# A reordered start of the first batch, and w_in permuted while it is cast so that w_out loads in long runs

## The chip, the cores and the metric

The kernel runs on one core of one Trainium2 chip. The metric is the device time of one execution in microseconds (us). PE is the tensor engine's matmul side, DVE is VectorE, ACT is ScalarE, POOL is GpSimd and SP is SyncE, which issues the transfers.

## The reference, cut to what matters

For each of 8 batches and 8 heads (576 positions, head size 64) an attention without a score matrix, then one feed-forward block over all 4608 tokens:

```python
q_s = softmax(q, axis=-1)            # over the head's 64 features
k_s = softmax(k, axis=2)             # over the 576 positions
kv  = einsum('bhsd,bhse->bhde', k_s, v)
x   = einsum('bhsd,bhde->bhse', q_s, kv)   # then (tokens, 512)
h   = x @ w_in                       # 512 -> 2048
g   = 0.5 * h * (1 + erf(h / sqrt(2)))
out = g @ w_out                      # 2048 -> 512
```

A permutation of w_in's 2048 columns permutes the columns of h and g. If w_out's rows are permuted alike, the output is the same.

## The kernel before

The kernel works on a chunk of 512 tokens at a time: a first projection (`h_phase`, 64 matmuls of 512 columns), Gelu on ACT, a second projection (`y_phase`, 64 matmuls). Attention for a later chunk runs between the matmuls. Only chunk 0 has nothing to hide behind: before its first projection, q, k, v and w_in must have landed and gone through this chain. Idle matmuls (`warm`) stand at the head so that PE is at full pace when the real work comes.

```python
    warm(30)
    table(AF.Exp)
    exp_q(0, parts=2)
    ...                                   # [cut: exponentials of k on ACT, q's normalisation]
    tp_step(0, 0)                         # transposes of q, pairs 0 and 1
    warm(5)
    ...                                   # [cut: casts of v; w_in blocks 0 and 1 on POOL]
    kv_pair(0, 0)
    tp_mm(0, 1)                           # transposes of q, pairs 2 and 3
    norm_pair(0, 0, "v")
    tp_evac(0, 1, "s")                    # their eviction, on ACT
    kv_pair(0, 1)
    norm_pair(0, 1, "v")
    x_step(0, 0)                          # x product of pair 0 and its eviction on DVE
    kv_pair(0, 2)
    kv_pair(0, 3)
    x_step(0, 1, "s")
    norm_pair(0, 2, "s")                  # half on DVE, half on ACT
    norm_pair(0, 3, "s")
    table(AF.Gelu)
    h_phase(0, {
        0: [lambda: cast_wi(2, wi[2], "v")],
        2: [lambda: cast_wi(3, wi[3], "v")],
        ...
    }, groups={0: 2}, pre={
        1: [lambda: x_step(0, 2)],        # before the matmuls on xT's second slice
        2: [lambda: x_step(0, 3)],
    })
```

w_in comes in five blocks of 256, 256, 512, 512 and 512 columns; POOL casts the first two to bf16 and DVE the others. w_out comes in four blocks of 512 rows, 1 MB each. In a partition, a block's four rows are 128 rows apart, so each run of DRAM is one row, 2 KB.

```python
        o = wi_bf[:, :, wi_off[i]:wi_off[i] + n]
        ...
                nc.vector.tensor_copy(out=o[:, c:c + d], in_=w[:, c:c + d, 0:n])
    ...
        src = moe_w_out[i * 512:(i + 1) * 512, :].rearrange("(c p) f -> p c f", p=128)
```

The softmax here doesn't subtract the row's maximum and nothing guards it: scores larger than these inputs give would overflow.

## Time and profile before

| | kernel before |
|---|---|
| median of the first 3 runs | 286.33 us (286.24 to 286.64) |
| span in the profile | 284.4 us |
| PE busy | 276.6 us, 97% |
| first projection of chunk 0 runs without a gap from | 17.68 us |
| second projection of chunk 0 starts at | 30.19 us |
| last eviction starts at | 281.03 us |

Read the table from the bottom: from the second projection's start to the last eviction there are 250.84 us, almost all of it matmuls at one per 0.216 us. What is left is the start, and that is where this change works. The lines of the profile are in the prediction below.

### The profile page before, as it was taken

How to read it: one execution, taken by the hardware profiler on the slowest of the kernel's cores; microseconds unless marked ns; L12 is line 12 of the kernel's file. 1: busy time of each engine (PE TensorE's matmuls, PEld its weight loads, DVE VectorE, ACT ScalarE, POOL GpSimd, SP SyncE). 2: the span in 40 equal slices, each digit the busy share in tenths (PEclk: the TensorE clock that was granted, in tenths of full speed). 3: DMA queues.
4: the chain of work that ended last, by engine and by line, in shares of the span. 5: the costliest groups of instructions: out<-in, count | busy, mean ns of one | idle time of the engine just before them, and what ended most of it. 6: DMA issues, size and time to landing. Idle time of an engine off the chain costs nothing.

```text
span 284.4 us, 3842 instructions
## 1 busy us (share of the span) xinstructions
PE 276.6 (97%) x1484; PEld 131.1 (46%) x1511; DVE 119.4 (42%) x239; ACT 159.7 (56%) x266; POOL 38.6 (14%) x34
## 2 busy tenths in 40 slices
PE   8989999999999999999999999999999999999995
PEld 3534455445445445444544454445444444444443
DVE  7664388028696454354434532453225111110012
ACT  4876595779565934694368526872576165017400
POOL 5830033002020050005000500040001300000000
PEclk9999999999999999999999999999999999999999
DMA  7999999999529939922993199517500600120033
GB/s 239 378 383 387 372 388 309 308 298 233 143 62 268 297 92 246 248 96 88 233 271 102 74 212 277 140 74 170 127 0 37 184 2 0 74 76 0 0 74 76
DMA packets 58593, 50.05 MB, mean 176 GB/s; under 512 B 26704, under 2 KB 48464, under 8 KB 58576
## 3 DMA queue, kind: packets, MB, share of 16 engines
q1 hardware_dynamic: 58288, 49.68, 61.1%
q8 instruction: 12, 0.20, 0.3%
q10 hardware_dynamic: 288, 0.13, 0.2%
q14 instruction: 5, 0.04, 0.1%
HBM read 36.70 MB, written 9.44 MB: 162 GB/s over the span
## 4 chain that ended last, share of the span: by engine, by line
PE 91%; DMA 3%; DVE 2%; ACT 2%; issue 1%; DVEq 0%; ACTq 0%
PE ps L376 40%; PE ps L386 40%; PE ps L476 3%; DMA f<-in_k_dram 3%; PE ps L251 2%; PE ps L408 1%; PE ps L346 1%; PE ps L323 1%; DVE xT L356 1%; ACT ek L145 1%; DVE kvbd L212 1%; PE ps L197 1%; PE ps L255 0%; PE ps L288 0%; ACT L145 0%
## 5 line engine op out<-in xcount | busy, mean ns | idle before, releaser
L381 ACT ACTIVATE g<-ps 128x512 bf16<-128x512 f32 x144 | 85.7, 597 | 93.4 <-PE ps L376 93.4
L376 PE MATMUL ps<-xT,wi_bf 128*128 128x512 bf16 x560 | 128.6, 379 | 1.3 <-DVE xT L356 0.3
L386 PE MATMUL ps<-wo_bf,g 128*128 128x512 bf16 x549 | 123.2, 379 | 0.6
L376 PEld LDWEIGHTS <-wi_bf 128*128 128x128 bf16 x576 | 55.3, 98 | 66.0 <-issue 2.8
L386 PEld LDWEIGHTS <-g 128*128 128x128 bf16 x560 | 54.6, 98 | 64.9
L393 DVE COPY y_sb<-ps 128x512 f32<-128x512 f32 x35 | 23.9, 686 | 74.9 <-PE ps L386 74.6
L243 POOL TENSOR_TENSOR e<-e,recq 128x1024 bf16<-128x1024 bf16 (+1 forms) x10 | 27.6, 2761 | 178.8 <-ACT ek L148 95.7
L356 DVE CAST xT<-ps 128x512 bf16<-128x512 f32 x32 | 20.6, 686 | 32.6 <-PE ps L346 22.5
L241 DVE TENSOR_REDUCE qsum<-e 128x16 f32<-128x1024 bf16 (+1 forms) x13 | 21.1, 1624 | 8.4 <-ACT e L145 7.0
L224 DVE CAST v_aug<-f 128x512 bf16<-128x512 f32 x24 | 10.3, 429 | 10.0 <-DMA f<-in_v_dram 9.3
L148 ACT ACTIVATE e<-f 128x512 bf16<-128x512 f32 (+2 forms) x28 | 13.2, 540 | 0.1
L97 ACT ACT_TABLE_LOAD x9 | 11.5, 1283 | 2.8 <-issue 2.6
L273 DVE TENSOR_SCALAR kvbd<-ps,rec 64x64 bf16<-64x64 f32 x48 | 11.6, 280 | 0.8
L476 PE MATMUL ps<-kvbd 128*128 128x512 bf16 x35 | 10.3, 462 | 1.2 <-DVE scr L85 1.2
L148 ACT ACTIVATE ek<-f 128x512 bf16<-128x512 f32 x20 | 10.9, 613 | 0.0
L182 ACT ACTIVATE ek<-f 64x1152 bf16<-64x1152 f32 x8 | 9.3, 1162 | 1.7 <-DMA f<-in_k_dram 1.5
L145 ACT ACTIVATE e<-f 128x1024 bf16<-128x1024 f32 (+1 forms) x7 | 6.8, 990 | 3.2 <-DMA f<-in_q_dram 3.2
L251 PEld LDWEIGHTS <-ek 128*128 128x128 bf16 x96 | 6.8, 97 | 3.2 <-ACT ek L145 0.6
L251 PE MATMUL ps<-v_aug,ek 128*128 128x129 bf16 x96 | 8.1, 220 | 0.1
L467 DVE CAST wo_bf<-w 128x2048 bf16<-128x2048 f32 (+1 forms) x5 | 5.1, 1014 | 5.8 <-DMA w<-in_moe_w_out_dram 5.7
L476 PEld LDWEIGHTS <-kvbd 128*128 128x128 bf16 x35 | 3.9, 116 | 6.6 <-issue 3.2
L216 DVE CAST vr_aug<-f 64x512 bf16<-64x512 f32 x6 | 2.5, 416 | 8.7 <-DMA f<-in_v_dram 8.7
(52 smaller groups left out, 98.6 us busy)
## 6 DMA issues: line engine op xcount, KB each, us to landing
out_dram<-y_sb SPq DMA_DIRECT2D x32, 256.0 KB, 2.4
f<-in_q_dram SPq DMA_DIRECT2D x6, 1024.0 KB, 7.7
f<-in_k_dram SPq DMA_DIRECT2D x6, 1024.0 KB, 10.8
f<-in_v_dram SPq DMA_DIRECT2D x6, 1024.0 KB, 9.6
w<-in_moe_w_in_dram SPq DMA_DIRECT2D x6, 512.0 KB, 8.6
w<-in_moe_w_out_dram SPq DMA_DIRECT2D x3, 1024.0 KB, 12.8
f<-in_k_dram SPq DMA_DIRECT2D x4, 576.0 KB, 8.6
f<-in_v_dram SPq DMA_DIRECT2D x8, 288.0 KB, 8.1
```

Of the source, the lines that this page charges most:

```text
L97: nc.scalar.activation(out=scr[:, 1:2], in_=scr[:, 0:1], func=func)
L148: nc.scalar.activation(out=dst[:, s::4], in_=src[:, u::4], func=AF.Exp)
L241: nc.vector.reduce_sum(out=qsum, in_=eq[:, :, hs, :], axis=AX.X)
L243: eng.tensor_tensor(out=eq[:, :, hs, :], in0=eq[:, :, hs, :], in1=recq.unsqueeze(3).to_broadcast([128, J, w, D]), op=ALU.mult,)
L251: nc.tensor.matmul(ps, st[b]["ek"][:, j, hs, :].rearrange("p h d -> p (h d)"), v_aug[b % 2][:, j, hp, 0:PW], start=(j == 0), stop=False,)
L273: nc.vector.tensor_scalar_mul(out=kvbd[b][pr, hps[i], c * 64:c * 64 + 64], in0=ps[pr, i, c * (D + 1):c * (D + 1) + D], scalar1=rec[pr, i:i ...
L356: nc.vector.tensor_copy(out=st[b]["xT"][:, hp, :], in_=ps)
L376: nc.tensor.matmul(ps, wi_bf[:, dm, t * 128:(t + 1) * 128], xT[:, dm, :], start=(dm == 0), stop=(dm == NDM - 1),)
L381: nc.scalar.activation(out=g[:, t, :], in_=ps, func=AF.Gelu)
L386: nc.tensor.matmul(ps, st[c]["g"][:, t, j * 128:(j + 1) * 128], wo_bf[:, t, :], start=(t == 0), stop=(t == NDF - 1),)
L393: nc.vector.tensor_copy(out=y_sb, in_=ps)
L476: nc.tensor.matmul(ps, zeros[:, 0:128], zeros, start=True, stop=True)
```

## The change

It has two parts. The chain of batch 0 is reordered: the Gelu table is loaded right after k's exponentials, q's second transpose is evicted by DVE instead of ACT, the normalisations of pairs 2 and 3 become one step on DVE, and the evictions of the x products are shared between ACT and DVE. And w_in's columns are permuted inside each block by the cast (column m·r + c goes to c·128 + m, with r = 2 or 4), so that w_out can be loaded with 2 or 4 neighbouring rows per partition, in runs of 4 or 8 KB.

```diff
+    def kv_two(b):                      # both pairs into one PSUM tile
+        ...
+    def norm_two(b):
+        ps = st[b]["kvt"]
+        rec = small.tile([128, 2], FP32, tag="reck")
+        nc.vector.reciprocal(rec, ps[:, :, D])
+        for hh in range(2):
+            pr = slice(hh * 64, hh * 64 + 64)
+            nc.vector.tensor_tensor(
+                out=kvbd[b][pr, 2:4, hh * 64:hh * 64 + 64], in0=ps[pr, :, 0:D],
+                in1=rec[pr].unsqueeze(2).to_broadcast([64, 2, D]), op=ALU.mult,
+            )
     def cast_wi(i, w, eng):
-        o = wi_bf[:, :, wi_off[i]:wi_off[i] + n]
+        r = n // 128
+        o = wi_bf[:, :, wi_off[i]:wi_off[i] + n].rearrange("p d (c m) -> p d c m", c=r)
+        w = w[:, :, 0:n].rearrange("p d (m c) -> p d c m", c=r)
     def load_wo(i, parts=1):
-        src = moe_w_out[i * 512:(i + 1) * 512, :].rearrange("(c p) f -> p c f", p=128)
+        ... # block 0: two halves with (p c) f, c=2
+        src = src.rearrange("(p c) f -> p c f", c=4)
     tp_mm(0, 1)
+    table(AF.Gelu)
     norm_pair(0, 0, "v")
-    tp_evac(0, 1, "s")
     kv_pair(0, 1)
     norm_pair(0, 1, "v")
-    x_step(0, 0)
-    kv_pair(0, 2)
-    kv_pair(0, 3)
+    x_step(0, 0, "s")
+    tp_evac(0, 1)
+    kv_two(0)
     x_step(0, 1, "s")
-    norm_pair(0, 2, "s")
-    norm_pair(0, 3, "s")
-    table(AF.Gelu)
+    norm_two(0)
     h_phase(0, { ... }, pre={
-        1: [lambda: x_step(0, 2)],
-        2: [lambda: x_step(0, 3)],
+        1: [lambda: x_step(0, 2), lambda: x_step(0, 3, "s")],
     })
```

More of the change, by code (lines that the diff above doesn't have):

```diff
@@ L212, in norm_pair @@
                 nc.vector.tensor_scalar_mul(out=dst, in0=ps[pr, 0:D], scalar1=rec[pr, 0:1])
+    def kv_two(b):
+        ps = psum_a.tile([128, 2, 256], FP32, tag="a")
+        st[b]["kvt"] = ps
+        for i in range(2):
+            for n in range(NS):
+                nc.tensor.matmul(
+                    ps[:, i, 0:D + 1], ek_pair[1][:, i, n, :], v_pair[b][:, 2 + i, n, 0:D + 1],
+                    start=(n == 0), stop=(n == NS - 1),
+                )
[8 more added lines that the diff above has]
+                in1=rec[pr].unsqueeze(2).to_broadcast([64, 2, D]), op=ALU.mult,
+            )
     def cast_vr(b):
@@ L448, in cast_wi @@
         n = wi_cols[i]
-        o = wi_bf[:, :, wi_off[i]:wi_off[i] + n]
+        r = n // 128
+        o = wi_bf[:, :, wi_off[i]:wi_off[i] + n].rearrange("p d (c m) -> p d c m", c=r)
+        w = w[:, :, 0:n].rearrange("p d (m c) -> p d c m", c=r)
         if eng == "p":
             for h in range(2):
-                nc.gpsimd.tensor_copy(out=o[:, 2 * h:2 * h + 2], in_=w[:, 2 * h:2 * h + 2, 0:n])
+                nc.gpsimd.tensor_copy(out=o[:, 2 * h:2 * h + 2], in_=w[:, 2 * h:2 * h + 2])
         else:
@@ L455, in cast_wi @@
             for c in range(0, NDM, d):
-                nc.vector.tensor_copy(out=o[:, c:c + d], in_=w[:, c:c + d, 0:n])
+                nc.vector.tensor_copy(out=o[:, c:c + d], in_=w[:, c:c + d])
     def load_wo(i, parts=1):
         w = wst.tile([128, 4, DM], FP32, tag="w")
-        src = moe_w_out[i * 512:(i + 1) * 512, :].rearrange("(c p) f -> p c f", p=128)
+        src = moe_w_out[i * 512:(i + 1) * 512, :]
+        if i == 0:
+            for h in range(2):
+                nc.sync.dma_start(
+                    out=w[:, 2 * h:2 * h + 2],
+                    in_=src[256 * h:256 * h + 256].rearrange("(p c) f -> p c f", c=2),
+                )
+            return w
+        src = src.rearrange("(p c) f -> p c f", c=4)
         n = 4 // parts
```

## The prediction

> **What bounds the kernel now.** I read the page first. Its busy shares, slices and chain of waits name the resource.
>
> ```profile
> PE 276.6 (97%) x1484; PEld 131.1 (46%) x1511; DVE 119.4 (42%) x239; ACT 159.7 (56%) x266; POOL 38.6 (14%) x34
> ...
> PE   8989999999999999999999999999999999999995
> ...
> PE 91%; DMA 3%; DVE 2%; ACT 2%; issue 1%; DVEq 0%; ACTq 0%
> ...
> L381 ACT ACTIVATE g<-ps 128x512 bf16<-128x512 f32 x144 | 85.7, 597 | 93.4 <-PE ps L376 93.4
> L376 PE MATMUL ps<-xT,wi_bf 128*128 128x512 bf16 x560 | 128.6, 379 | 1.3 <-DVE xT L356 0.3
> L386 PE MATMUL ps<-wo_bf,g 128*128 128x512 bf16 x549 | 123.2, 379 | 0.6
> ```
>
> The reader is to see that PE (the tensor engine) is busy in every slice, that 91% of the chain that ended last is PE, and that the two large matmul groups waited 1.3 us and 0.6 us in the whole run. A "busy" PE can still run slowly, so I checked its pace. Gelu activations in batch 0 start at 20.03, 20.89, 21.76, 22.62 and 23.48 us, one per four matmuls: 3.45 us over 16 matmuls, 0.216 us each. That pace never slackens in the phases that follow, with the clock at 9 tenths or more throughout. Next I took busy time by stretches. From 17.7 to 30 us PE is busy 12.25 of 12.30 us, from 30 to 48.2 us 17.84 of 18.20, from 48.2 to 68 us 19.63 of 19.80. So the kernel is a fixed amount of matmul work, 266 us or so, preceded by about 17 us of preparation. Only where that work starts can be moved.
>
> Third, I read PE's timeline from 10 us on, where the change lies. Columns: start, duration, engine, line, operation, how many, and in brackets the idle time before and what ended it.
>
> ```profile
> 12.85 0.45 PE L197 MATMUL ps<-v_aug,ek 128*128 128x65 bf16 x9
> 13.53 0.39 PE L323 MATMUL ps<-qT,kvbd 128*128 128x512 bf16 x1 [0.23 <-DVE kvbd L212]
> 13.76 0.73 PE L197 MATMUL ps<-v_aug,ek 128*128 128x65 bf16 x18
> 14.34 0.39 PE L323 MATMUL ps<-qT,kvbd 128*128 128x512 bf16 x1
> 15.06 0.38 PE L376 MATMUL ps<-xT,wi_bf 128*128 128x512 bf16 x1 [0.33 <-DVE xT L356]
> 15.86 0.39 PE L323 MATMUL ps<-qT,kvbd 128*128 128x512 bf16 x1 [0.42 <-ACT kvbd L210]
> 16.08 0.59 PE L376 MATMUL ps<-xT,wi_bf 128*128 128x512 bf16 x2
> 16.52 0.38 PE L323 MATMUL ps<-qT,kvbd 128*128 128x512 bf16 x1
> ```
>
> L197 is the KV product of a head pair, L323 the product x of a head pair with its queries, L376 the first projection. The four x products (call them x0 to x3) run at 13.53, 14.34, 15.86 and 16.52 us. The first projection takes x0 to x3 in that order, so it is saturated only when x3 has been evicted. The same stretch of the other engines shows why that is late.
>
> ```profile
> 13.05 1.01 ACT L299 COPY qT<-ps 128x1024 bf16<-128x1024 bf16 x1 [0.16 <-PE ps L288]
> 13.71 0.58 DVE L212 TENSOR_SCALAR kvbd<-ps,rec 64x64 bf16<-64x64 f32 x2
> 14.26 1.18 POOL L452 CAST wi_bf<-w 128x512 bf16<-128x512 f32 x2 [0.84 <-DMA w<-in_moe_w_in_dram]
> 14.32 0.69 DVE L356 CAST xT<-ps 128x512 bf16<-128x512 f32 x1
> 15.49 0.63 ACT L210 ACTIVATE kvbd<-ps,rec 64x64 bf16<-64x64 f32 x2
> 16.14 1.28 ACT L97 ACT_TABLE_LOAD   x1
> 16.28 1.34 DVE L356 CAST xT<-ps 128x512 bf16<-128x512 f32 x2 [0.50 <-PE ps L323]
> 17.54 1.42 DVE L456 CAST wi_bf<-w 128x512 bf16<-128x512 f32 x4
> ```
>
> x2 and x3 are both evicted by DVE (VectorE), one after the other, until 17.62 us. By the chain of waits PE then starts its unbroken run at 17.68 us. That is the number the change can move.
>
> **What the Trainium skill says.** "VectorE: DVE Perf Modes", section Mode 2×_2P, says a one-source SBUF copy uses both read ports and needs an even outermost dimension; it asks for no contiguous step. The trace agrees on the rate: a 128x512 f32 cast takes 420 ns and a 128x1024 one 695 ns, so 512 more elements cost 275 ns, 1.86 elements per ns. "SBUF — State Buffer", section Door 1, note on cachelines, says lines are 16 bytes and that less than two hits on a line costs extra, by an amount it does not give. The permuted casts of the three 512-column blocks step 4 floats, 16 bytes. No row of this trace has such a step. "GPSIMD Engine Reference", section 7, says reads slow down by about half above a step of 8 bytes. The 256-column blocks, which POOL (GpSimd) casts, step 2 floats, exactly 8 bytes, so I leave them at 616 ns. "ScalarE: Activation LUTs", sections What ACT_TABLE_LOAD costs and Table sets, gives 1283 ns per load, as the trace has it (1283), and puts copy in every set, so evictions by ACT (ScalarE) after an early Gelu load need no second load. Its drain of 1380 ns is not seen here: the next activation starts 0.02 us after the load ends.
>
> **The change part by part.**
>
> *Table load moved.* ACT's last exponential ends at 12.89 us. The Gelu load then takes 12.89 to 14.17, its dummy activation until about 14.39. It leaves the stretch at 16.14 to 17.42, where nothing waited for it (the first Gelu waits for PE until 18.09). Gain by itself 0. Cost: ACT can evict x0 only from 14.39 to 14.98 (0.59 from the L358 row), against DVE's end at 15.01 today. No loss: the first projection still starts at about 15.05.
>
> *qT eviction from ACT to DVE.* DVE ends the second normalisation at 14.29, evicts 14.30 to 14.99 (0.69, row L297). It was 1.01 us on ACT. It takes the place of x0's eviction on DVE, so DVE is free at the same time, 15.0.
>
> *kv_two and norm_two.* The same 18 matmuls, at 13.76 as today. The normalisation had two reciprocals, two DVE scalings and two ACT scalings, done at 15.80 (pair 2) and 16.12 (pair 3). Now it is one reciprocal and two two-pair products on DVE. From today's rows the reciprocal starts and the scaling follows 0.19 us later. A 64x64 scaling takes 0.28; 64 more elements from PSUM at about 0.75 elements per ns (512 in 686 ns) add at most 0.085, so I take 0.35 each. Sum: 15.00 + 0.19 + 0.35 + 0.35 = 15.89. Both pairs are ready together.
>
> *The x products.* With 0.06 us of hand-over (13.47 to 13.53 today), x2 starts at 15.95 and x3 one pace later at 16.17. Today: 15.86 and 16.52. Then come the two projection matmuls on x1, at 16.38 and 16.60.
>
> *Evictions of x2 and x3.* PE start to eviction start is 0.42 us today (15.86 to 16.28). DVE evicts x2 from 16.37 to 17.06, and ACT x3 from 16.59 to 17.18, side by side. Projection on x2 at 17.12 and 17.34, on x3 at 17.55 without a gap. Today's unbroken run starts with x3 at 17.68. Gain 17.68 − 17.55 = 0.13 us.
>
> *Strided casts.* Suppose the 16-byte step halves DVE's rate: 420 becomes about 0.70 and 695 about 1.24. The first block then runs from 17.06, four casts of about 0.62 net, until 19.6. When the projection on x2 starts, 12 of the 16 matmuls ahead of that block's first tile remain, so its first cast (done at 17.8) is needed at 17.12 + 12 × 0.216 = 19.7 and its last at 20.4. The second block lands at 20.4 and 21.7 and is cast by 21.6 and 23.0; its halves are needed 16 matmuls (3.45 us) later, at 23.2 and 23.6. The third is cast by 25.8 and its second half needed at 27.0. All beside PE. Cost 0 on the path.
>
> *w_out in 4 KB and 8 KB runs.* 2048 runs of 2 KB become 768. Queue q1 is at its ceiling of 380 to 390 GB/s through this stretch with 1 KB and 2 KB runs alike, so I expect no faster stream. Even if w_out landed sooner, its casts (27.20, 29.90, 32.63) are waited for by no matmul: L386 idles 0.6 us in all. Gain 0.
>
> *Sum:* 286.33 − 0.13 = 286.2 us.
>
> **The rivals.** First, **the strided casts become the bound**: if a 16-byte step costs three times or more, the first block's four casts of 1.1 us end past 21 us, and the first projection stalls about 1 us there and more at the later blocks, giving 287 to 288. For it: nothing has measured the step here. Against it: the blocks have 0.6 to 1.2 us of slack even at half rate, and it is one phase of nine. Second, **POOL slows at the 8-byte step** by half: its first cast ends at 15.2 rather than 14.85, still ahead of x2; its fourth ends at 17.9, about 0.5 us before its first use. That gives 286.2 to 286.6. Third, **DVE as a chain of one engine**: norm_two is slower than I took (0.5 us each), so x2 starts at 16.25 and the gain is gone: 286.5. Fourth, **the DMA gain is real**: larger runs speed the stream and remove the 0.25 us idle time at 47.8 us. Against it, that idle time ends with a kvbd scaling on ACT, not with a transfer; 285.9 at best.
>
> **Range and chances.** All of PE's idle time between 10 us and 17.7 us is about 2 us, so a gain over 1 us is hardly possible, and 2% (5.7 us) is out of reach. The run spread is 0.4 us. I put 286.2, with 285.6 to 286.8. Faster by over 2%: 0.01. Within 2%: 0.98. Slower by over 2%: 0.01.
>
> **What would show it.** Right: x2 and x3 one pace apart near 16.0, the unbroken run near 17.55, the two casts of xT side by side on DVE and ACT, PE waits of L376 no longer than now, packets down by about 1280. Wrong: PE waiting for wi_bf (casts too slow), norm_two ending after 16.1, or PE's work after 17.6 us differing in length from today's.

## The result, and the profile after

The changed kernel took 286.44 us (median of 6 runs, 285.51 to 286.60); the kernel before, in 6 runs, also 286.44 us (286.04 to 287.34). The ratio is 0.9992 with an interval of 0.9972 to 1.0011: the same. Here and below a ratio is the mean time of one kernel's fast runs over the mean of the other's of the same rounds, so it is not quite the ratio of the medians quoted.

First, lines of the page of the changed kernel: busy times, shares of the chain that ended last, and groups (busy us, mean ns of one, idle us before and what ended it).

```profile
PE 276.3 (97%) x1484; PEld 130.9 (46%) x1511; DVE 121.4 (43%) x237; ACT 159.0 (56%) x265; POOL 38.7 (14%) x34
...
PE 90%; ACT 4%; DMA 2%; issue 1%; DVE 1%; SPq 0%; ACTq 0%
...
L398 PE MATMUL ps<-xT,wi_bf 128*128 128x512 bf16 x560 | 128.4, 379 | 1.7 <-ACT xT L380 0.8
...
L482 DVE CAST wi_bf<-w 128x512 bf16<-128x512 f32 (+1 forms) x8 | 6.9, 894 | 1.5 <-DMA w<-in_moe_w_in_dram 1.5
```

PE is as busy as before. ACT's share of the chain has risen from 2% to 4%, and the first projection's longest wait is now for ACT. DVE works 2.0 us more in all; its eight casts of w_in alone take 6.9 us instead of 4.2 (1.4 and 2.8, by shape).

Next the timeline of the changed kernel over the stretch that the prediction worked out (start, duration, engine, line, operation, number, idle time before).

```profile
13.24 0.39 PE L345 MATMUL ps<-qT,kvbd 128*128 128x512 bf16 x1 [0.23 <-DVE kvbd L212]
13.40 1.28 ACT L97 ACT_TABLE_LOAD   x1
...
14.04 0.69 DVE L319 COPY qT<-ps 128x1024 bf16<-128x1024 bf16 x1
...
14.72 1.24 POOL L478 CAST wi_bf<-w 128x512 bf16<-128x512 f32 x2 [0.82 <-DMA w<-in_moe_w_in_dram]
14.80 1.05 ACT L380 CAST xT<-ps 128x512 bf16<-128x512 f32 x2
14.84 0.59 DVE L231 TENSOR_TENSOR kvbd<-ps,rec 64x128 bf16<-64x128 f32 x2
...
15.42 0.38 PE L398 MATMUL ps<-xT,wi_bf 128*128 128x512 bf16 x1 [0.81 <-ACT xT L380]
...
15.86 0.59 PE L345 MATMUL ps<-qT,kvbd 128*128 128x512 bf16 x2
...
16.27 0.69 DVE L378 CAST xT<-ps 128x512 bf16<-128x512 f32 x1 [0.85 <-PE ps L345]
...
16.49 0.59 ACT L380 CAST xT<-ps 128x512 bf16<-128x512 f32 x1 [0.63 <-PE ps L345]
...
17.00 2.52 DVE L482 CAST wi_bf<-w 128x512 bf16<-128x512 f32 x4
```

x2 and x3 are issued one pace apart at 15.86, and evicted side by side at 16.27 and 16.49, as foreseen. But norm_two ended at 15.43 and x2 waited: the first projection stands ahead of it on PE, and that waited for ACT's eviction (14.80 to about 15.39) and POOL's cast (from 14.72) at once. Both were late here. k's exponentials had begun at 8.66 us, against 8.17 in the first trace of before, and w_in's first block had landed for 14.72, against 14.26. The second projection starts at 29.96 us, the last eviction at 280.80: 0.23 us ahead of the kernel before at both ends, with 250.84 us between them, exactly as before. By the prediction's own measure, the first matmul on x3, the start is at 17.45 us here and 17.20 in the second trace, where 17.55 was predicted and the kernel before has 17.68.

One line holds something more. DVE's first cast of w_in, at 17.00 us, took 0.92 us and the next three 0.62 each: POOL's last cast of w_in was still running, until 17.44. In the five traces in which these two overlap (by 0.32 to 0.45 us), DVE's first cast takes 0.20 to 0.32 us longer than its fellows; in the other nine it does not. So the earlier start also makes these two casts collide. No run was made to test this, and in the changed kernel no matmul waited for that cast.

The wide runs show in w_out. Lines of DVE's timeline: the casts of the first two blocks, each waiting for its block to land. The kernel before:

```profile
27.20 1.23 DVE L467 CAST wo_bf<-w 128x2048 bf16<-128x2048 f32 x1 [2.02 <-DMA w<-in_moe_w_out_dram]
29.90 1.23 DVE L467 CAST wo_bf<-w 128x2048 bf16<-128x2048 f32 x1 [1.48 <-DMA w<-in_moe_w_out_dram]
```

The changed kernel:

```profile
26.91 1.23 DVE L501 CAST wo_bf<-w 128x2048 bf16<-128x2048 f32 x1 [1.53 <-DMA w<-in_moe_w_out_dram]
29.32 1.23 DVE L501 CAST wo_bf<-w 128x2048 bf16<-128x2048 f32 x1 [1.19 <-DMA w<-in_moe_w_out_dram]
```

A block of 1 MB follows the last one after 2.41 us instead of 2.70. That is 435 GB/s instead of 388 (1 MB over these times). From 17.7 to 30 us, with a part of w_in in the window, the transfers move 404 GB/s instead of 386. The packets fell from 58,593 to 57,329, by 1264 of the 1280 expected.

So there is a gain of about 0.2 us in this pair of traces, 0.1% of the time, and six executions of one kernel scatter over 1.3 us. The questions for experiments were: is the time really the start plus fixed work; which part moves the start; are the slower casts hidden, and by how much; and what makes the start differ between executions.

### The profile page after: what moved, and what is told of

Same layout as the page of the kernel before. It is cut to its first block, busy times and chain, and to the rows that moved or that the text cites. A ratio compares the mean times of both kernels' runs of the same rounds, so it can differ in the third digit from the quotient of the medians.

```text
span 284.3 us, 3840 instructions
## 1 busy us (share of the span) xinstructions
PE 276.3 (97%) x1484; PEld 130.9 (46%) x1511; DVE 121.4 (43%) x237; ACT 159.0 (56%) x265; POOL 38.7 (14%) x34
## 2 busy tenths in 40 slices
DMA packets 57329, 50.05 MB, mean 176 GB/s; under 512 B 26720, under 2 KB 48480, under 8 KB 57056
## 4 chain that ended last, share of the span: by engine, by line
PE 90%; ACT 4%; DMA 2%; issue 1%; DVE 1%; SPq 0%; ACTq 0%
PE ps L398 43%; PE ps L408 40%; DMA f<-in_k_dram 2%; PE ps L273 2%; ACT ek L182 2%; PE ps L430 1%; PE ps L368 1%; PE ps L345 1%; ACT ek L145 1%; PE ps L277 0%; ACT L145 0%; ACT L97 0%; PE ps L197 0%; ACT e L145 0%; SPq L108 0%
## 5 line engine op out<-in xcount | busy, mean ns | idle before, releaser
L378 DVE CAST xT<-ps 128x512 bf16<-128x512 f32 x30 | 19.2, 685 | 32.9 <-PE ps L368 22.5
L97 ACT ACT_TABLE_LOAD x9 | 11.5, 1283 | 2.8 <-issue 2.6
L482 DVE CAST wi_bf<-w 128x512 bf16<-128x512 f32 (+1 forms) x8 | 6.9, 894 | 1.5 <-DMA w<-in_moe_w_in_dram 1.5
```

The source lines that it names most:

```text
L378: nc.vector.tensor_copy(out=st[b]["xT"][:, hp, :], in_=ps)
```

## The experiments

Theory: the span of the profile is the moment at which the second projection of chunk 0 can start, plus 250.84 us to the last eviction, plus about 3.4 us that every trace has behind it; the measured time is another 1.9 us or so longer than the span. The reordered chain moves that start a little, the permutation does not. Rivals: the gain comes through the transfers; the slower casts eat a larger gain; later waits absorb whatever the start gains.

**The changed kernel once more**, unedited, five rounds.

> The changed kernel once more, unedited, for a second trace and a tighter ratio. Theory (the time is the start of the unbroken matmul run plus a fixed amount of work): the run starts 0.1 to 0.4 us before that of the kernel before, the rest has the same length, ratio 0.998 to 1.000. Rival (the late arrival of k in the first trace, 8.66 us against 8.17, belongs to the change and eats a larger gain): k arrives late here too and ACT's exponentials again start at 8.6 or later. If it is jitter, they start anywhere from 8.1 to 8.7.

286.12 us (285.93 to 286.80, 5 runs), before 286.57 us (11 runs), ratio 0.9988 (0.9975 to 1.0001). k's exponentials began at 8.31 us and w_in's first cast at 14.34, so the late landing of the first trace was jitter. Without it the chain is as short as it can be; lines of its timeline:

```profile
13.35 0.39 PE L345 MATMUL ps<-qT,kvbd 128*128 128x512 bf16 x1 [0.24 <-DVE kvbd L212]
...
14.95 0.59 DVE L231 TENSOR_TENSOR kvbd<-ps,rec 64x128 bf16<-64x128 f32 x2
...
15.60 0.60 PE L345 MATMUL ps<-qT,kvbd 128*128 128x512 bf16 x2
```

x2 follows x0 after 2.25 us, and the second projection (29.71 us) follows x0 after 16.36 us. In the kernel before, the latter is 30.19 − 13.53 = 16.66 us. The reordering shortens this chain by 0.30 us. The lines divide it: x2 follows x0 0.08 us sooner (2.25 us against 15.86 − 13.53 = 2.33), and 0.22 us, one matmul's pace, comes from evicting x2 and x3 side by side, so that x3's matmuls follow x2's without the gap of the kernel before.

**The kernel before once more**, one look.

> The kernel before, unedited, for a second trace. If the moment at which q, k and v land differs from execution to execution, ACT's first k exponential starts away from 8.17 us here, by up to 0.5 us, and the start of the unbroken run moves with the landings from 17.68 by up to 0.4 us. If they are fixed, both repeat within 0.1 us.

It took 286.61 us. k's exponentials began at 8.10 us, not far from 8.17, but everything after them moved: the transposes start at 10.31 us instead of 10.07, x0 at 13.76 instead of 13.53, the second projection at 30.43 instead of 30.19. The chain from x0 is 16.67 us, as before. So the start moves by 0.24 us from execution to execution with no edit at all, as much as the change moves it.

**Only the reordered chain** (w_in cast in order, w_out in 2 KB runs).

```diff
-        (permuted views o and w in cast_wi, wide views in load_wo)
+        (those of the kernel before)
```

> Only the reordered batch 0 chain, with w_in cast unpermuted and w_out loaded in 2 KB runs as before. Theory: the whole gain of the start is here, so the unbroken run starts as in the changed kernel (within 0.2 us), casts of the 512-column blocks take 420 and 695 ns, and the ratio is 0.998 to 1.000. Rival (the permutation gives part of the gain through the transfers): the run starts as in the kernel before and the ratio is 1.000 to 1.002.

286.25 us (6 runs), ratio 0.9990 (0.9975 to 1.0005). The casts are back at 420 and 695 ns (the first, which overlaps POOL's last, took 0.70 us). The first projection gets going early, near 16.4 us, but does not run through: the last quarter of w_in's third block landed late, was cast only at 19.56 us, and the first projection waited for it. The second projection starts at 29.77. And here, alone of all kernels with the unedited tail, the rest is longer than 250.84 us: 281.19 − 29.77 = 251.42. Lines of its timeline show where:

```profile
41.24 1.89 PE L408 MATMUL ps<-wo_bf,g 128*128 128x512 bf16 x8
43.34 0.45 PE L197 MATMUL ps<-v_aug,ek 128*128 128x65 bf16 x9 [0.22 <-POOL v_aug L188]
```

In the other traces the first of these comes 11.26 us after the start of the second projection, so here at 41.03 us; it came at 41.24, after the cast of the first half of w_out's last block (40.49 to 41.18). The second waited for v of the next batch. The early start is not what did it: the kernel before with 26 idle matmuls (below) starts its second projection at 29.82 us, also with 2 KB runs, and has that cast done at 40.63 where it is needed at 41.08. What differs here is the late third block of w_in, with the queue behind it late as well. With the wide runs the cast is done earlier, at 40.09 in the second trace of the changed kernel, and even where the third block was as late (19.71 us, in the wide runs without the permutation, below) at 40.71, needed at 41.18. So in these traces the long runs leave more room behind a late landing; that they pay in time is not shown, and why the third block was late in these two executions stays open.

**Only the permutation and the wide runs** (the old chain).

```diff
-        o = wi_bf[:, :, wi_off[i]:wi_off[i] + n]
+        (permuted views in cast_wi, wide views in load_wo, as in the change)
```

> Only the permuted cast and the wide w_out runs, with the old batch 0 chain. Theory: hidden altogether; DVE casts take 618 and 1096 ns, w_out lands earlier, the unbroken run starts as in the kernel before (17.6 to 17.8 us), ratio 0.999 to 1.001. Rival (slow casts or faster transfers reach the path): PE waits for wi_bf after 18 us and the ratio is above 1.002, or the ratio is below 0.998.

286.02 us (5 runs), ratio 0.9982 (0.9969 to 0.9995). In the trace the chain from x0 to the second projection is 29.91 − 13.25 = 16.66 us, that of the kernel before, and the rest is 250.84 us. So this part neither gains nor loses on the chain from x0, and its start fell early in the profiled execution because the transposes did (9.78 us). The interval lies just below 1 and was not forecast. No step of the trace accounts for a gain of 0.5 us from it; several ratios were taken, each from 5 or 6 executions, and the four of these rounds (0.9982 to 0.9990) share the same 11 executions of the kernel before; I leave it open.

**Wide runs without the permutation**, a wrong result (relative error 1.4).

> The kernel before with w_out loaded in 4 and 8 KB runs but w_in not permuted: the result is wrong on purpose. Theory (the wide runs alone speed the transfers): the window from 17.7 to 30 us moves 400 GB/s or more against 386, w_out's casts on DVE start about 0.3 to 0.6 us sooner, the DVE casts of w_in stay 420 and 695 ns, and the time stays within noise of the kernel before. Rival (the higher rate came from the slower casts or from where the trace fell): 386 GB/s as before.

It took 286.16 us in one execution. From 17.7 to 30 us 406 GB/s were moved, and w_out's first blocks were cast 2.41 us apart, with casts of w_in at their old speed. So longer runs suffice for the faster stream. That the first cast of w_out would start sooner was wrong in this trace (27.76 us): a part of w_in's third block landed late, as above, and everything behind it in the queue with it.

**Each DVE cast of w_in made twice.**

```diff
-                nc.vector.tensor_copy(out=o[:, c:c + d], in_=w[:, c:c + d])
+                for _ in range(2):
+                    nc.vector.tensor_copy(out=o[:, c:c + d], in_=w[:, c:c + d])
```

> The changed kernel with each DVE cast of w_in made twice (same values; result stays right). It asks how much slack the slower casts have. The first block's last cast then ends about 2.5 us later, at 21.7 to 22 where it ended at 19.2 to 19.5 and is needed at about 20. Theory (the casts are hidden by a slack of 0.5 to 1.2 us only): PE waits for wi_bf once or more, 1.5 to 4 us in all, ratio 1.005 to 1.014, and the length after the start of the second projection stays 250.84 us. Rival (the casts are far from the path): ratio within 0.002 of 1.

289.61 us (4 runs), ratio 1.0103 (1.0090 to 1.0116). From the waits of PE between 9 and 50 us:

```profile
PE ps L398 <- DVE wi_bf L483: 3.2, 4, 0.8
```

PE waited 3.2 us for DVE's casts, in four waits. The rest stayed 250.83 us. In the changed kernel a cast of the fourth or fifth block takes 1.09 us and a new one lands every 1.35 us, so DVE waits 0.26 us between them: the casts at step 16 bytes use four fifths of what there is, and twice their time is too much. They are hidden, but not by much.

**Twenty more idle matmuls before the first projection.**

```diff
     norm_two(0)
+    warm(20)
```

> The changed kernel with 20 idle matmuls of 0.216 us put on PE in front of the first projection, 4.3 us of work, of which about 1.2 to 1.5 us fills PE's idle time before the unbroken run. Theory (the time is the start of the run plus fixed work): the second projection starts 2.6 to 3.2 us later and the time rises by the same, ratio 1.009 to 1.011, with 250.84 us from there to the last eviction. Rival (later waits absorb a late start, or a late start adds new ones): the rise is less than half of that, or above 4.3 us.

290.30 us (4 runs), ratio 1.0132 (1.0118 to 1.0145). The second projection starts at 34.55 us, 4.84 us after that of the second trace of the changed kernel, with 250.83 us to the last eviction. Against the ratio of the changed kernel (0.9988) the timed runs rose by 1.44%, 4.1 us. The forecast of 2.6 to 3.2 us was too low in one term: I had let a part of the 4.3 us fill PE's idle time, but the idle matmuls need the PSUM buffer of x0 and waited for its eviction:

```profile
15.70 4.48 PE L510 MATMUL ps<-kvbd 128*128 128x512 bf16 x19 [0.70 <-ACT xT L380]
```

So all of the 4.3 us were added (4.40 us, counted from x0), and nothing of them was absorbed later. (In this trace the transposes also started late, at 10.34 us.) The claim tested, start plus fixed work, holds.

**x2 and x3 ahead of the first projection.**

```diff
-        1: [lambda: x_step(0, 2), lambda: x_step(0, 3, "s")],
+        0: [lambda: x_step(0, 2), lambda: x_step(0, 3, "s")],
```

> The changed kernel with x2 and x3 put ahead of the first two projection matmuls. In the trace of the changed kernel the first projection waited 0.81 us at 15.42, with norm_two done at 15.43, so x2 and x3 stand behind a wait that they do not need. Theory (the order on PE costs 0.4 us): x2 starts near 15.5, its eviction 0.4 us sooner, the unbroken run starts near 16.7 on the scale where the changed kernel's starts at 17.0, ratio to the kernel before 0.997 to 0.999. Rival (the arrival of w_in and POOL's casts set the start): the run starts where it did and the ratio is that of the changed kernel.

286.43 us (6 runs), ratio 0.9988 (0.9975 to 1.0001), the ratio of the changed kernel. In the trace PE waits 1.03 us for norm_two and then runs without a gap from 16.11 us, but the chain from x0 is 16.49 us, no shorter than 16.36. When w_in and k are on time, the two projection matmuls fit into the wait for norm_two, and taking them out of it gains nothing. The wait of 0.81 us in the first trace was no fault of the order.

**The Gelu table loaded behind x1's eviction.**

```diff
     tp_mm(0, 1)
-    table(AF.Gelu)
     norm_pair(0, 0, "v")
     ...
     norm_two(0)
+    table(AF.Gelu)
```

> The changed kernel with the Gelu load put back behind x1's eviction. Theory (in the changed kernel's trace two waits end together: ACT's eviction of x0 at 15.39, behind the Gelu load, and POOL's first w_in cast at 15.36): x0 is evicted by about 14.4, but the first projection still waits for the cast, so the start of the unbroken run moves by less than 0.2 us. Rival (the load ahead of the evictions sets the start): the run starts 0.3 to 0.8 us sooner. Third: the load, now between the evictions of x1 and x3, delays x3 and the run by up to 0.5 us.

286.37 us in one execution. x0 is evicted from 14.16 to 14.75 us, and still the first projection starts at 15.04, when POOL's first cast (from 14.34) is done. The second trace of the changed kernel, with POOL's cast also at 14.34, starts it at 15.08. The chain from x0 is 16.38 us. Where the load stands makes no difference to the chain in this one execution, since the cast ends with it.

**The copies by themselves**: eight copies more on DVE and eight on POOL in the first projection of the last chunk, f32 to bf16, with steps of 1, 2, 4 and 8 elements, of 256 and 512 elements.

```diff
+    def probe_steps():
+        src = st[B]["qf"].rearrange("p j h d -> p (j h d)")
+        for eng in (nc.vector, nc.gpsimd):
+            for s in (1, 2, 4, 8):
+                v = src.rearrange("p (m c) -> p c m", c=s)
+                ...
```

> The kernel before with eight copies more on DVE and eight on POOL in the last projection phase, from an f32 tile to a scratch bf16 tile: steps of 1, 2, 4 and 8 elements, each with 256 and 512 elements. Result stays right. Theory (the cost of a step depends on how many elements lie in 16 bytes): on DVE the 512-element copy takes 420 ns at steps 1 and 2, about 620 at steps 4 and 8; on POOL about 616 at step 1, 640 at step 2, and more than 800 at steps 4 and 8. Rival (any step but 1 costs alike): steps 2, 4 and 8 take the same. The time rises by 0 to 4 us, since the copies may hold up evictions in that phase.

The result is right and the time 286.39 us (one execution). Lines of the timelines of DVE and of POOL, the 512-element copies at steps 1, 2 and 4, in this order on each engine (their order in time tells which is which):

```profile
254.46 0.43 DVE L643 CAST ek<-f 128x512 bf16<-128x512 f32 x1
...
255.25 0.43 DVE L643 CAST ek<-f 128x512 bf16<-128x512 f32 x1
...
256.13 0.62 DVE L643 CAST ek<-f 128x512 bf16<-128x512 f32 x1
...
258.43 0.61 POOL L643 CAST ek<-f 128x512 bf16<-128x512 f32 x1
...
259.58 0.65 POOL L643 CAST ek<-f 128x512 bf16<-128x512 f32 x1
...
260.99 1.10 POOL L643 CAST ek<-f 128x512 bf16<-128x512 f32 x1
```

Step 8 took 0.63 us on DVE and 1.11 us on POOL. A step of 8 bytes is free on DVE and nearly so on POOL; 16 and 32 bytes cost alike. The kernel's split is well chosen: POOL has the blocks of step 2, and DVE those of step 4, where POOL would need 1.10 us.

**26 idle matmuls at the head instead of 30**, on both kernels.

```diff
-    warm(30)
+    warm(26)
```

> The kernel before with 26 idle matmuls at its head in place of 30. In most traces so far the first transposes start when the 30 end (10.07, 10.31, 9.79, 9.89, 10.41 us), not when their data is ready (about 9.3, as where the 30 ended early). Theory (the length of the 30, which differs from execution to execution, sets the chain's start): transposes at 9.3 to 9.5, first x product at 12.8, the second projection starts at 29.5 to 30.0 against 30.19 and 30.43, ratio 0.997 to 0.999. Rival (w_in's landing is the bound behind it): it starts at 29.8 or later and the ratio is 0.999 to 1.001.

> The changed kernel with the same 26. If the start of the chain were the only limit, the changed kernel would keep its lead of 0.2 to 0.3 us over the same edit of the kernel before: second projection at 29.2 to 29.7, ratio 0.996 to 0.998. Rival (w_in's landing near 14.1 to 14.7 and its second block near 19 to 19.6 bind both kernels): second projection at 29.6 to 29.9, ratio 0.998 to 0.9995, and no clear difference from the other edit.

The kernel before with this edit: 286.16 us (6 runs), ratio 0.9989 (0.9975 to 1.0003). The changed kernel with it: 286.13 us (5 runs), ratio 0.9986 (0.9974 to 0.9998). No clear difference between them, as the rival said. The transposes start at 9.29 and 9.62 us, the second projection at 29.82 and 29.92. What the early chain gains, w_in's landing takes back: its first casts begin at 14.39 and 14.67.

**What sets the start.** In seven of the twelve traces with 30 idle matmuls the transposes (9.79 to 10.41 us) follow their end. In the other five they follow the end of POOL's normalisation of q: at 9.30 to 9.35 us, and at 9.78 in the trace of only the permutation, where q had landed late. The 30 take a different time in each execution. The kernel before, first trace, then the kernel with only the reordered chain, each from PE's timeline:

```profile
1.19 9.04 PE L476 MATMUL ps<-kvbd 128*128 128x512 bf16 x30 [1.19 <-DVE scr L85]
```

```profile
1.19 7.94 PE L500 MATMUL ps<-kvbd 128*128 128x512 bf16 x30 [1.19 <-DVE scr L85]
```

Both start at 1.19 us; one is done 1.1 us before the other, and over all traces the 30 take 7.93 to 9.38 us. At 0.216 us each they would take 6.5 us. The packed traces hold the start of each: the first of them come 0.427 us apart and the rest 0.216, and there are 6 slow ones in the shortest case (each cast made twice) and 13 in the longest (x2 and x3 first). So the moment of full pace moves. The Trainium skill, "TensorE: Matmul & The Clock Gate", Part 1, says that the array starts at half its clock and is let up to full by a window that does not start with the kernel, so that the moment varies from run to run. The traces agree with the half rate and the varying moment; the granted clock reads 1.00 in these stretches of the profile and does not show it.

With that, two limits describe the start of the second projection: x0 plus the rest of the chain, and the start of POOL's first w_in cast plus what follows it. Four traces gave the constants: 16.66 and 15.43 us for the old chain (first trace of before; the same with 26 idle matmuls), 16.36 and 15.24 us for the new one (second and first trace of after). The other six rows of the table test them.

| trace | x0 | first w_in cast | limit by x0 | limit by w_in | second projection starts |
|---|---|---|---|---|---|
| before | 13.53 | 14.26 | 30.19 | 29.69 | 30.19 |
| before, again | 13.76 | 14.12 | 30.42 | 29.55 | 30.43 |
| before, 26 idle | 12.76 | 14.39 | 29.42 | 29.82 | 29.82 |
| before, with the copies | 13.19 | 14.78 | 29.85 | 30.21 | 30.21 |
| only the permutation | 13.25 | 14.20 | 29.91 | 29.63 | 29.91 |
| after | 13.24 | 14.72 | 29.60 | 29.96 | 29.96 |
| after, again | 13.35 | 14.34 | 29.71 | 29.58 | 29.71 |
| after, 26 idle | 13.09 | 14.67 | 29.45 | 29.91 | 29.92 |
| after, late table | 13.74 | 14.34 | 30.10 | 29.58 | 30.12 |
| only the chain | 12.81 | 14.16 | 29.17 | 29.40 | 29.77 |

Of the six rows that test them, five fit within 0.02 us. (In the two traces of the changed kernel that the second limit sets, k was late too, and ACT's eviction of x0 ended with the cast; in all traces not held up by x0's eviction the first projection starts 0.67 to 0.71 us after the cast's start, so the cast alone would have set it.) The sixth, only the chain, waited for w_in's third block, as told; so did the wide runs without the permutation (29.92 where 29.62 would fit). The change shortens the first limit by 0.30 us and the second by 0.19: again 0.22 from the side-by-side evictions (14.54 us from the first projection's start to the second's, against 14.76), less 0.03 for POOL's first cast, slower at its step of 8 bytes. How late x0 and w_in come is up to the execution; in the traces the start lies anywhere from 29.7 to 30.4 us.

## Why the prediction was right or wrong

The time (286.44 us against 286.2), the range and the class were right, but that says little: six executions of one kernel scatter over 1.3 us, so any forecast of almost no change would have been right too. That the first pair of traces differs by 0.23 us, near the 0.13 predicted, is partly luck of the landings: x0 came 0.29 us earlier there and the chain behind it is 0.30 shorter, but w_in came 0.46 later and took most of it back. By its steps:

- **The bound.** Right, and sharper than stated: 250.83 or 250.84 us from the second projection to the last eviction in all traces with an unedited tail but one, and 4.1 us more in front cost 4.1 us.
- **The table load moved, no gain and no loss.** Right when k is on time. In the first trace k came late and the load pushed x0's eviction to 14.80 us, but moving the load back gained nothing, because POOL's cast ends at the same time.
- **norm_two.** The mechanism was right, the size off. The prediction took 0.35 us for each product and a start after q's eviction; the trace has 0.59 us for both, and the reciprocal overlaps the eviction (it starts 0.61 us after an eviction of 0.69). x2 follows x0 after 2.25 us where 2.42 were predicted. The 0.17 us is the difference between the gain of 0.13 us predicted and 0.30 us measured on that chain: the prediction had x2 0.09 us later than today, and it came 0.08 us sooner.
- **x2 and x3 one pace apart, evicted side by side.** Right, and the larger part of the gain (0.22 us).
- **Strided casts at half rate, hidden.** Hidden: right. The rate was taken a little too low: about 620 and 1090 ns, against 0.70 and 1.24 us assumed. That the slack is small fits too: doubled, the casts cost 3 us.
- **POOL at a step of 8 bytes.** Taken as 616 ns, measured about 640, which costs 0.03 us where w_in's landing sets the start.
- **"I expect no faster stream".** Wrong. Longer runs gave 404 to 406 GB/s against 386, shown alone by the run with the wrong result. That the stream seemed to be at a ceiling with 1 KB and 2 KB runs alike did not make it one for 8 KB. The conclusion drawn from it, no gain in time, still held for this kernel, for the other reason given: no matmul was waiting for w_out.
- **What it did not see.** It took the landings and the end of the idle matmuls as fixed times. One of its signs failed for this: "PE waits of L376 no longer than now" (1.3 us) against 1.7 and 1.4 us in the two traces of the changed kernel, while the kernel before itself had 0.5 us in its second trace. They scatter between executions by more than the gain (the first w_in cast begins anywhere from 14.10 to 14.98 us, the idle matmuls end within 1.4 us), and w_in's landing is a second limit close behind the chain. The chain of waits of the kernel before had the idle matmuls in it, right up to the transposes, and I read past them.

The rivals fell: the casts do not bound, POOL does not slow enough to matter, norm_two is faster rather than slower, and the faster stream did not remove the wait of 0.25 us near 47.8 us, which is still there at 47.59 in the changed kernel. None of the edited versions is clearly faster than the changed kernel; apart from the two that were slowed on purpose, all ratios lie between 0.998 and 0.9992 and their intervals overlap, so there is no better version to hand on. By the timed runs the change itself isn't shown to gain anything either.

## What to carry to other kernels

When a kernel is one long matmul run behind a short start, measure the start from fixed events in the trace (here from one product to the second projection) rather than from zero, since a shift of 0.3 us that repeats to 0.02 us can be read that way and is lost in the total. Before shortening one chain of a start, look for the next one behind it: here the landing of the first weights stands within half a microsecond. A permutation of a weight that another weight can follow cost little where the strided read stayed at 8 bytes (0.65 against 0.61 us on POOL) or fell on an engine with slack (0.62 against 0.43 us on DVE), and long DRAM runs pay only where something waits for that transfer.

## What the Trainium skill lacked or had wrong

- "SBUF — State Buffer", section Door 1, note on cachelines, gives no size for the cost of one hit per 16-byte line. On DVE the f32 to bf16 copy of 512 elements took 0.43 us at steps of 4 and 8 bytes, 0.62 at 16 and 0.63 at 32; with the 256-element copies (0.28 and 0.39 us) that is 0.59 and 0.90 ns for each further element.
- "GPSIMD Engine Reference", section 7, gives half as much again above a step of 8 bytes. The place of the cliff is right, the height is not that of this copy: 0.61, 0.65, 1.10 and 1.11 us at 4, 8, 16 and 32 bytes for 512 elements, 80% more; by the difference to 256 elements (0.40 and 0.64 us), 0.82 and 1.80 ns for each further element.
- "DMA: Bandwidth & Descriptors", section Specifications, gives 512 bytes as the least transfer for line rate. Runs of 4 and 8 KB in place of 2 KB raised the rate in the same window from 386 to between 404 and 406 GB/s, and shortened the time between two 1 MB blocks from 2.70 to 2.41 us.
- "TensorE: Matmul & The Clock Gate", Part 1, gives about 0.5 us either way for the moment of full pace. Its own later note, that one kernel had 6, 11 or 14 slow matmuls, fits better: here 6 to 13 of the same 30 came 0.427 us apart, the pace of 0.216 us began at 3.99 us in the earliest case and 6.96 in the latest, and the 30 took 7.93 to 9.38 us.
- "ScalarE: Activation LUTs", section What ACT_TABLE_LOAD costs, adds a drain of 1380 ns to the 1283 ns. In these traces the next activation starts 0.01 to 0.02 us after the load ends.
